# Attention decode on one Trainium2 core: keys loaded by pairs of units in 64 KB rows, at alternating offsets in one buffer

## The chip, the cores and the metric

The kernel runs on one core of one Trainium2 chip. The metric is the device time of one execution in microseconds; the kernel before takes 630.53 us (median of 3 runs, 630.49 to 630.74). A core has TensorE (PE; its weight loads are shown as PEld), VectorE (DVE), ScalarE (ACT), GpSimd (POOL) and SyncE (SP), and 16 DMA engines that move data between the chip's main memory (DRAM, HBM) and SBUF. TensorE writes into PSUM, from where VectorE and ScalarE read.

## The reference

One query for each of 32 heads attends over 65,536 keys; four query heads share one of 8 key/value heads. All tensors are bfloat16.

```python
B, Hq, Hkv, Sq, Sk, D = 1, 32, 8, 1, 65536, 128
...
def reference(q, k, v):
    B, Hq, Sq, D = q.shape
    Hkv = k.shape[1]
    rep = Hq // Hkv
    k = jnp.repeat(k, rep, axis=1)
    v = jnp.repeat(v, rep, axis=1)
    scale = D ** -0.5
    scores = jnp.einsum("bhqd,bhkd->bhqk", q, k) * scale
    p = _softmax(scores, axis=-1)
    return jnp.einsum("bhqk,bhkd->bhqd", p, v)
```

Keys and values are 134 MB each, and each is read once.

## The kernel before

A **unit** is a quarter of a head's keys: 128 x 128 = 16,384 keys, held as T = 128 tiles of 128 keys. There are NU = 32 units. A **round** handles two units, a (even) and b (odd), half a head; there are NR = 16 rounds, 0 to 15. In DRAM the 32,768 keys of a round are laid out so that each of the 128 partitions owns 256 consecutive keys, which are 64 KB in a row; unit a takes the first 32 KB of each partition's row and unit b the second.

**Loads (SP).** Keys go to two buffers of 128 tiles, `kbuf0` for a and `kbuf1` for b, by one DMA of 4 MB for each unit (128 rows of 32 KB; `load_k`, L406). Values of a whole round go to `vbuf` by one DMA of 8 MB (128 rows of 64 KB; `load_v`, L416). The order in SP's queue is: keys a, keys b, values, round after round. Before keys of a buffer are loaded again, SP waits for `kfree[b]`, which VectorE or ScalarE raises when it comes to the unit's last eviction (L204); before values it waits for `vfree`, raised when a round's values are summed (L298). The first unit's keys come in two halves, the values of round 14 and the keys of round 15 in halves, and the very last values in pieces (`V_PIECES`).

**Keys on TensorE.** For each group of TB = 8 tiles TensorE transposes the tiles into one of four PSUM buffers `trb` (`pe_transposes`, L117); the group is copied (evicted) to `ktb` in SBUF, three groups of four by VectorE and every fourth by ScalarE (`on_act`, L27; `evict`, L199); then 8 matmuls make its scores in `qkb` with the four queries as the moving operand (`pe_scores`, L128). Scores run LAG = 3 groups behind the transposes. A unit has G = 16 groups; TensorE waits for `krdy` ahead of a unit's first tile and for `khalf` at its middle.

**Softmax.** When a unit's scores are done (`qkd`), VectorE takes the maximum over its tiles (`scores_done`, L229), GpSimd reduces it over the partitions (L389), VectorE forms the running maximum (`maximum`, L239), and ScalarE makes four exponentials of 128 columns, one for each query head, with their sums, into `pts` (`exponentials`, L345). `exd` tells TensorE, and `sx` VectorE, that they are there. After a head's last unit VectorE first copies the next head's queries (`next_queries`).

**Values on TensorE.** For each unit 128 matmuls accumulate values times `pts` (`pe_values`, L158). TensorE's order in a round is: keys a, keys b, values a, values b (L190). VectorE rescales the accumulator `acc` by `alpha` and adds (L261 to L271), once for each unit. The round's order on VectorE is written out in `dve_round` (L273), on ScalarE in `act_round` (L358).

The last unit's values stand in `pe_last` (L165): they come in pieces; between them the sum over `lp` is taken, and then the last four rows are divided and stored.

Of the kernel before, what the change touches and what calls it, by code (L numbers as in the profile page):

```python
# [10 lines left out]
P = 128  # L11
T = 128
TB = 8
G = T // TB
# [4 lines left out]
HALF = T // 2  # L19
# [3 lines left out]

LOOP_SLOT = 176
# [18 lines left out]
def bass_standalone__gqa_softmax__decode_kernel(nc, q, k, v, out):  # L43
# [7 lines left out]

    NR, HALVES = NU // 2, HU // 2
    kf, vf, qf, of = k[0], v[0], q[0, :, 0, :], out[0, :, 0, :]
# [29 lines left out]
    rsum = sb("rsum", [P, R], DT.float32)  # L83
# [14 lines left out]
    fin = pvb[NU % 2]  # L98
# [18 lines left out]
    def pe_transposes(pe, b, j):  # L117
        kv = kbuf[b][:, :].rearrange("p (t d) -> p t d", d=D)
        for i in range(TB):
            t = j * TB + i  # L120
            if t == 0:
                take(pe, krdy[b], 16)
            if t == HALF:
                take(pe, khalf[b], 16)
            ins = pe.transpose(trb[j % NTB][:, i * P:(i + 1) * P], kv[:, t, :], ident[:, :])  # L125
        ins.then_inc(tra if on_act(j) else trd, 1)

    def pe_scores(pe, b, j):  # L128
        done, (k, last) = eva if on_act(j) else evd, turn(j)
        if j == 0:  # L130
            take(pe, qrdy)
        if last:
            take(pe, done, k)
        for i in range(TB):
            t, off = j * TB + i, (j % NKG * TB + i) * P
            ins = pe.matmul(qkb[b][:, t * R:(t + 1) * R], lhsT=ktb[:, off:off + P],  # L136
                            rhs=qcur[:, :], start=True, stop=True)
# [5 lines left out]
    def pe_keys(pe, b):  # L143
        pend = []
        for j in range(G):
            pe_transposes(pe, b, j)
            pend.append(j)
            if len(pend) > LAG:
                pe_scores(pe, b, pend.pop(0))
        while pend:  # L150
            pe_scores(pe, b, pend.pop(0))

    def value(pe, b, t, first, last):
        vv = vbuf[:, :].rearrange("p (t d) -> p t d", d=D)
        return pe.matmul(pvb[b][:, 0:R], lhsT=vv[:, b * T + t, :], rhs=pts[b][:, t * R:(t + 1) * R],  # L155
                         start=t == first, stop=t == last)

    def pe_values(pe, b):  # L158
        take(pe, vrdy[b], 16)
        take(pe, exd)  # L160
        for t in range(T):
            ins = value(pe, b, t, 0, T - 1)
        ins.then_inc(pvd, 1)

    def pe_last(pe):  # L165
        b = (NU - 1) % 2
        starts = [sum(V_PIECES[:i]) for i in range(len(V_PIECES))]
        pe.wait_ge(t_o, H - 1)
        pe.transpose(qkb[0][0:HR - R, 0:P], oT[:, R:HR], identf[:, :]).then_inc(s_o, 1)
        take(pe, exd)  # L170
        for t in range(T):
# [4 lines left out]
            ins = value(pe, b, t, 0, T - 1)  # L176
# [5 lines left out]
        ins.then_inc(s_fin, 1)  # L182

    def tensor_engine(pe):
# [14 lines left out]
    def evict(e, n, j):  # L199
        dst = ktb[:, j % NKG * TB * P:(j % NKG + 1) * TB * P]  # L200
        k, last = turn(j)
        if last:
            take(e, tra if on_act(j) else trd, k)
        if j == G - 1:  # L204
            e.sem_inc(kfree[n % 2], 1)
# [4 lines left out]
        if not last:  # L210
            ins.wait_op(tra if on_act(j) else trd, k, "sem-ge")
# [10 lines left out]
    PART = [[j for j in range(a, b) if not on_act(j)] for a, b in ((0, 4), (4, 12), (12, G))]  # L222

    def evictions(e, n, parts):
        for part in parts:
            for j in part:
                evict(e, n, j)

    def scores_done(e, u):  # L229
# [4 lines left out]
        else:  # L234
# [15 lines left out]
    def add_sums(e, u):  # L250

        take(e, sx)
        if u % HU == 0:
            own(e, e.tensor_copy(lp[:, :], rsum[:, :]), xd)
# [10 lines left out]
    def add_values(e, u):  # L265
        take(e, pvd)
        pv = pvb[u % 2][:, 0:R]
        if u % HU == 0:
            own(e, e.tensor_copy(acc, pv), xd)  # L269
        else:  # L270
            own(e, e.tensor_tensor(acc, acc, pv, ALU.add), xd)  # L271
# [24 lines left out]
    def values_done(e, u):  # L296
        add_values(e, u)
        e.sem_inc(vfree, 1)  # L298
# [23 lines left out]
    def vector_engine(e):  # L322
# [7 lines left out]
        with e.Fori(0, H) as h:  # L330
            for i in range(HALVES):
                dve_round(e, i, h)
        e.sem_inc(t_lp, 1)
        e.wait_ge(s_o, 1)
# [3 lines left out]
        ins = e.tensor_tensor(acc, acc, pvb[(NU - 1) % 2][:, 0:R], ALU.add)  # L338
# [6 lines left out]
    def exponentials(e, u):  # L345

        take(e, ng)
        e.activation(alpha[u % 2][:, :], dm[:, :], AF.Exp, scale=scale)  # L348
        sv = qkb[u % 2][:, :].rearrange("p (t g) -> p g t", g=R)
        pv = pts[u % 2][:, :].rearrange("p (t g) -> p g t", g=R)  # L350
        for g in range(R):
            ins = e.activation(pv[:, g, :], sv[:, g, :], AF.Exp, bias=negm[:, g:g + 1],  # L352
                               scale=scale, accum_out=rsum[:, g:g + 1])
# [4 lines left out]
    def act_round(e):  # L358
        for j in (3, 7, 11, 15):
            evict(e, 0, j)  # L360
        evict(e, 1, 3)
        exponentials(e, 0)
        for j in (7, 11, 15):
            evict(e, 1, j)
        exponentials(e, 1)

    def scalar_engine(e):
# [3 lines left out]
        with e.Fori(0, NR):  # L371
            act_round(e)
# [24 lines left out]
    def sync_engine(e):  # L397
        kp, vp, w = pairs(kf), pairs(vf), T * D

        def pieces(buf, s, sizes, sems):  # L400
            a = 0
            for n, sm in zip(sizes, sems):
                e.dma_start(buf[:, a * D:(a + n) * D], s[:, a * D:(a + n) * D]).then_inc(sm, 16)  # L403
                a += n

        def load_k(i, b, halves, first=False):  # L406
            if not first:
                take(e, kfree[b])
            s = kp[i][:, b * w:(b + 1) * w]
            if halves:  # L410
                pieces(kbuf[b], s, (HALF, T - HALF), (krdy[b], khalf[b]))
            else:
                e.dma_start(kbuf[b][:, :], s).then_inc(krdy[b], 16)
                e.sem_inc(khalf[b], 16)

        def load_v(i):  # L416
            e.dma_start(vbuf[:, :], vp[i]).then_inc(vrdy[0], 16)
            e.sem_inc(vrdy[1], 16)

        load_k(0, 0, True, first=True)  # L420
        load_k(0, 1, False, first=True)
        load_v(0)
        with e.Fori(1, NR - 2) as i:
# [55 lines left out]
```

## Time and profile before

| | |
|---|---|
| median of 3 runs | 630.53 us |
| the profiled execution | 630.56 us, its span (first to last instruction) 628.5 us |
| data read | 268.44 MB, 427 GB/s over the span |
| TensorE busy (matmul / weight load) | 78% / 77% of the span |
| VectorE, ScalarE, GpSimd busy | 50%, 30%, 3% |
| mean granted TensorE clock | 0.79 |

The head of the profile gives each engine's share of the span. Views by time list instructions merged: start in us from the span's start, duration in us, engine, source line, operation, output and input, count, and in square brackets the idle time of the engine ahead of it with what ended it. Views by group have total busy time and the mean of one in ns. The view of DMA issues has, for the issues of a stretch, size and median time from issue to landing. Windows give, for a stretch of time, the busy time of PE, PEld, DVE, ACT and POOL, the granted clock, the busy share of the DMA engines and GB/s. PEq, DVEq and so on are an engine's sequencer; L40 is the helper that waits for a semaphore.

### The profile page before, as it was taken

The numbers are of one execution on the slowest core, as the hardware profiler recorded it, in microseconds if no ns is written. First come the engines' busy times: TensorE is split into PE (matmuls) and PEld (weight loads), VectorE is DVE, ScalarE is ACT, GpSimd is POOL, SyncE is SP. The second block draws the span as 40 slices with busy tenths as digits, with TensorE's granted clock in tenths as the row PEclk, the third lists the DMA queues.
The fourth block names the chain that finished last, engine by engine and source line by source line (L and its number), as shares of the span: only waits on it lengthen the run. The fifth ranks groups of instructions, "written<-read, shape, count | busy, mean of one in ns | idle before, by whom it ended". The sixth has DMA issues, their size and how long they took to land. (4 is left out here: it accounts for less than half of the span.)

```text
span 628.5 us, 27046 instructions
## 1 busy us (share of the span) xinstructions
PE 489.2 (78%) x12293; PEld 482.3 (77%) x12293; DVE 312.5 (50%) x693; ACT 186.6 (30%) x418; POOL 16.4 (3%) x50
## 2 busy tenths in 40 slices
PE   4868859788696877967779686895868949689897
PEld 4758859687696877967679686895868949689896
DVE  4534726447273462725627256371563716537373
ACT  2321413314142141422414224041241413414141
POOL 0000000000000000000000000000000000000000
PEclk9776958769597695967959689696886969869596
DMA  8999999999999999999999999999999999999996
GB/s 369 439 426 446 434 415 453 415 453 430 419 448 419 448 419 434 453 413 455 407 432 438 425 438 430 430 455 409 455 413 438 442 415 448 417 434 432 423 444 283
DMA packets 8458, 268.58 MB, mean 427 GB/s; under 512 B 1026, under 2 KB 1282, under 8 KB 1538
## 3 DMA queue, kind: packets, MB, share of 16 engines
q1 hardware_dynamic: 8360, 268.44, 99.2%
q8 instruction: 7, 0.11, 0.1%
q10 hardware_dynamic: 90, 0.02, 0.0%
q14 instruction: 1, 0.01, 0.0%
HBM read 268.44 MB, written 0.01 MB: 427 GB/s over the span
## 5 line engine op out<-in xcount | busy, mean ns | idle before, releaser
L125 PE MATMUL trb<-ident,kbuf 128*128 128x128 bf16 x4096 | 328.3, 233 | 42.7 <-PEq L40 42.7
L209 DVE COPY ktb<-trb 128x1024 bf16<-128x1024 bf16 x384 | 254.2, 689 | 100.8 <-PE trb L125 97.5
L125 PEld LDWEIGHTS trb<-ident,kbuf 128*128 128x128 bf16 x4096 | 262.8, 105 | 43.7 <-issue 43.7
L207 ACT ACTIVATE ktb<-trb 128x1024 bf16<-128x1024 bf16 x128 | 131.1, 1024 | 379.1 <-PE trb L125 320.0
L136 PE MATMUL qkb<-qcur,ktb 128*128 128x4 bf16 x4096 | 170.9, 165 | 21.9 <-PEq L40 21.9
L136 PEld LDWEIGHTS qkb<-qcur,ktb 128*128 128x128 bf16 x4096 | 153.3, 97 | 26.0 <-issue 23.9
L155 PE MATMUL pvb<-pts,vbuf 128*128 128x4 bf16 x4096 | 112.3, 166 | 68.7 <-PEq L40 57.9
L155 PEld LDWEIGHTS pvb<-pts,vbuf 128*128 128x128 bf16 x4096 | 111.1, 104 | 70.1 <-issue 68.5
L352 ACT ACTIVATE pts<-qkb,negm 128x128 bf16<-128x128 f32 x128 | 50.5, 540 | 0.0
L236 DVE TENSOR_REDUCE cmax<-qkb 128x4 f32<-128x512 f32 x32 | 22.1, 692 | 43.2 <-DVEq L40 42.0
L271 DVE TENSOR_TENSOR acc<-acc,pvb 128x4 f32<-128x4 f32 x23 | 3.6, 158 | 62.8 <-DVEq L40 62.8
L352 ACT ACTIVATION_READ_ACCUMULATOR pts<-qkb,negm 128x1 f32 x128 | 34.6, 270 | 0.0
L389 POOL PARTITION_ALL_REDUCE cmaxa<-cmax x32 | 11.9, 372 | 576.3 <-POOLq L40 576.3
L348 ACT ACTIVATE alpha<-dm 128x4 f32<-128x4 f32 x32 | 6.6, 205 | 54.2 <-ACTq L40 53.4
L256 DVE TENSOR_TENSOR lp<-lp,alpha 128x4 f32<-128x4 f32 x24 | 3.8, 160 | 34.2 <-DVEq L40 34.2
L269 DVE COPY acc<-pvb 128x4 f32<-128x4 f32 x8 | 1.3, 162 | 25.5 <-DVEq L40 25.5
L246 DVE TENSOR_TENSOR m<-m,cmaxa 128x4 f32<-128x4 f32 x24 | 3.8, 159 | 11.5 <-DVEq L40 11.5
L218 DVE COPY qcur<-qT 128x4 bf16<-128x4 bf16 x9 | 1.5, 169 | 13.4 <-DVEq L40 13.3
L263 DVE TENSOR_TENSOR acc<-acc,alpha 128x4 f32<-128x4 f32 x24 | 3.9, 163 | 4.3 <-DVEq L40 1.9
L247 DVE TENSOR_TENSOR dm<-m 128x4 f32<-128x4 f32 x24 | 3.9, 162 | 3.5
L257 DVE TENSOR_TENSOR lp<-lp,rsum 128x4 f32<-128x4 f32 x24 | 3.9, 162 | 3.5
L391 POOL PARTITION_ALL_REDUCE la<-lp x8 | 3.4, 431 | 29.3 <-POOLq L40 29.3
(42 smaller groups left out, 23.7 us busy)
## 6 DMA issues: line engine op xcount, KB each, us to landing
kbuf<-in_k_dram SPq DMA_DIRECT2D x29, 4096.0 KB, 26.0
kbuf<-in_k_dram SPq DMA_DIRECT2D x6, 2048.0 KB, 21.1
vbuf<-in_v_dram SPq DMA_DIRECT2D x3, 4096.0 KB, 24.9
vbuf<-in_v_dram SPq DMA_DIRECT2D x1, 2048.0 KB, 29.4
vbuf<-in_v_dram SPq DMA_DIRECT2D x1, 1024.0 KB, 31.4
vbuf<-in_v_dram SPq DMA_DIRECT2D x1, 512.0 KB, 32.2
vbuf<-in_v_dram SPq DMA_DIRECT2D x1, 320.0 KB, 32.5
vbuf<-in_v_dram SPq DMA_DIRECT2D x14, 30.9
```

The costliest lines, as they stand in the source:

```text
L125: ins = pe.transpose(trb[j % NTB][:, i * P:(i + 1) * P], kv[:, t, :], ident[:, :])
L136: ins = pe.matmul(qkb[b][:, t * R:(t + 1) * R], lhsT=ktb[:, off:off + P], rhs=qcur[:, :], start=True, stop=True)
L155: return pe.matmul(pvb[b][:, 0:R], lhsT=vv[:, b * T + t, :], rhs=pts[b][:, t * R:(t + 1) * R], start=t == first, stop=t == last)
L207: ins = e.activation(dst, trb[j % NTB][:, :], AF.Copy).then_inc(eva, 1)
L209: ins = e.tensor_copy(dst, trb[j % NTB][:, :]).then_inc(evd, 1)
L236: e.tensor_reduce(cmax[:, :], qkb[u % 2][:, :].rearrange("p (t g) -> p g t", g=R), AX.X, ALU.max).then_inc(cm, 1)
L247: e.tensor_tensor(dm[:, :], mo[:, :], mn[:, :], ALU.subtract)
L257: own(e, e.tensor_tensor(lp[:, :], lp[:, :], rsum[:, :], ALU.add), xd)
L263: own(e, e.tensor_tensor(acc, acc, alpha[u % 2][:, :], ALU.mult), xd)
L348: e.activation(alpha[u % 2][:, :], dm[:, :], AF.Exp, scale=scale)
L352: ins = e.activation(pv[:, g, :], sv[:, g, :], AF.Exp, bias=negm[:, g:g + 1], scale=scale, accum_out=rsum[:, g:g + 1])
L389: e.partition_all_reduce(cmaxa[:, :], cmax[:, :], P, bass.bass_isa.ReduceOp.max).then_inc(cma, 1)
```

## The change

Keys of a round are loaded by one DMA of 8 MB with rows of 64 KB, as values were already, in rounds 1 to 13. The two key buffers become one `kbuf` of 320 tiles (T = 128, C = 64: 2T + C). Even rounds lie at tiles 64 to 319, odd rounds at 0 to 255. The 192 tiles 64 to 255 are common to both offsets. They are worked on first (GC = 24 groups); the other 64 tiles, at the end of an even round's stretch or at the beginning of an odd one's, come last, in 8 groups, by one of two branches on the round's parity. When the last common group is transposed, `kfree` lets SP load the next round's keys over them, at the other offset.

So that an odd round works on the common tiles first, its tiles are taken in a rotated order: `row_tile` gives the place in the row of the x-th tile, (x + 64) mod 256. Unit a of an odd round is places 64 to 191, unit b is places 192 to 255 and then 0 to 63, whose exponentials are made in two parts of 64 columns with sums of their own. `pts` is one buffer in the order of the row; values are accumulated by quarters q of 64 tiles into four column groups of `pvb[0]`, in the order 1, 0, 2, 3, where quarter 1 waits for the exponentials of a and quarter 0 for those of b. VectorE adds four quarters, with the rescale for b between them, and then raises `vfree`.

The groups of a round are counted through, G = 32. TensorE transposes groups 0 to 23 with scores three groups behind, finishes those scores, then transposes groups 24 to 31 (each from 28 on waits until the `trb` buffer is evicted) and then makes their scores. VectorE's maximum of unit a follows its evictions of groups 24 to 26, ScalarE's exponentials of a its eviction of group 27, ahead of group 31.

Round 0's keys come in parts of 64, 64 and 128 tiles, round 14's in two of 128, round 15's in four of 64; the values of round 14 come in halves and the last ones in a half and the same pieces as before. `pe_last` has the values of both units of round 15. The place of TensorE's loop in its code (`LOOP_SLOT`) changes from 176 to 80.

Bodies that are replaced stand in the listing of the kernel above.

```diff
+C = 64
...
-G = T // TB
+G = 2 * T // TB
+GA = T // TB
+GC = 3 * C // TB
...
-HALF = T // 2
...
-LOOP_SLOT = 176
+LOOP_SLOT = 80
...
+    def row_tile(odd, x):
+        return (x + C) % (2 * T) if odd else x
...
-    kbuf = [sb(f"kbuf{i}", [P, T * D], DT.bfloat16) for i in range(2)]
+    kbuf = sb("kbuf", [P, (2 * T + C) * D], DT.bfloat16)
...
-    pts = [sb(f"pts{i}", [P, T * R], DT.bfloat16) for i in range(2)]
+    pts = sb("pts", [P, 2 * T * R], DT.bfloat16)
...
-    rsum = sb("rsum", [P, R], DT.float32)
+    rsum = [sb(f"rsum{i}", [P, R], DT.float32) for i in range(3)]
...
-    krdy = [sem(f"krdy{i}") for i in range(2)]
-    khalf = [sem(f"khalf{i}") for i in range(2)]
...
+    krdy = [sem(f"krdy{i}") for i in range(2 * T // C)]
...
-    kfree = [sem(f"kfree{i}") for i in range(2)]
-    vfree = sem("vfree")
+    kfree, vfree = sem("kfree"), sem("vfree")
...
-    def pe_transposes(pe, b, j):
-        kv = kbuf[b][:, :].rearrange("p (t d) -> p t d", d=D)
+    def pe_transposes(pe, j, first):
+        if j * TB % C == 0:
+            take(pe, krdy[j * TB // C], 16)
...
+            t = first + i
+            ins = pe.transpose(trb[j % NTB][:, i * P:(i + 1) * P], kbuf[:, t * D:(t + 1) * D],
+                               ident[:, :])
+            if i == 0 and j >= GC + NTB:
+                ins.wait_op(eva if on_act(j - NTB) else evd, turn(j - NTB)[0], "sem-ge")
...
-    def pe_scores(pe, b, j):
+    def pe_scores(pe, j):
...
-            t, off = j * TB + i, (j % NKG * TB + i) * P
-            ins = pe.matmul(qkb[b][:, t * R:(t + 1) * R], lhsT=ktb[:, off:off + P],
+            t, off = (j * TB + i) % T, (j % NKG * TB + i) * P
+            ins = pe.matmul(qkb[j // GA][:, t * R:(t + 1) * R], lhsT=ktb[:, off:off + P],
...
-        if j == G - 1:
+        if j % GA == GA - 1:
...
+    def pe_keys(pe, i):
+        for j in range(GC + LAG):
+            if j < GC:
+                pe_transposes(pe, j, C + j * TB)
+            if j >= LAG:
+                pe_scores(pe, j - LAG)
+        with pe.If(i % 2 < 1):
+            for j in range(GC, G):
+                pe_transposes(pe, j, C + j * TB)
+        with pe.If(i % 2 > 0):
+            for j in range(GC, G):
+                pe_transposes(pe, j, j * TB - 3 * C)
+        for j in range(GC, G):
+            pe_scores(pe, j)
+    def value(pe, out, r, first, last):
+        return pe.matmul(out, lhsT=vbuf[:, r * D:(r + 1) * D], rhs=pts[:, r * R:(r + 1) * R],
+                         start=first, stop=last)
+    def pe_values(pe):
+        for q in (1, 0, 2, 3):
+            if q in (1, 2):
+                take(pe, vrdy[q - 1], 16)
+            if q in (1, 0):
+                take(pe, exd)
+            for r in range(q * C, (q + 1) * C):
+                ins = value(pe, pvb[0][:, q * R:(q + 1) * R], r, r % C == 0, r % C == C - 1)
+        ins.then_inc(pvd, 1)
+    def pe_last(pe):
+        starts = [sum(V_PIECES[:i]) for i in range(len(V_PIECES))]
...
+        pe.wait_ge(vrdy[0], 16)
+        for x in range(T):
+            ins = value(pe, pvb[0][:, 0:R], row_tile(True, x), x == 0, x == T - 1)
+        ins.then_inc(pvd, 1)
...
-            ins = value(pe, b, t, 0, T - 1)
+            ins = value(pe, pvb[1][:, 0:R], last_tile(t), t == 0, t == T - 1)
...
+    def last_tile(t):
+        return t if t < C else 2 * T - 2 * C + t
     def tensor_engine(pe):
...
-            pe_keys(pe, 0)
-            pe_keys(pe, 1)
-            pe_values(pe, 0)
+            pe_keys(pe, i)
...
-                pe_values(pe, 1)
+                pe_values(pe)
...
-    def evict(e, n, j):
+    def evict(e, j):
...
-        k, last = turn(j)
+        (k, last), done = turn(j), tra if on_act(j) else trd
...
-            take(e, tra if on_act(j) else trd, k)
-        if j == G - 1:
-            e.sem_inc(kfree[n % 2], 1)
+            take(e, done, k)
+        if j == GC - 1:
+            e.wait_ge(done, k)
+            e.sem_inc(kfree, 1)
...
-        if not last:
-            ins.wait_op(tra if on_act(j) else trd, k, "sem-ge")
+        if not last and j != GC - 1:
+            ins.wait_op(done, k, "sem-ge")
     def own(e, ins, s):
...
-    PART = [[j for j in range(a, b) if not on_act(j)] for a, b in ((0, 4), (4, 12), (12, G))]
...
+    def evictions(e, a, b):
+        for j in range(a, b):
+            if not on_act(j):
+                evict(e, j)
     def scores_done(e, u):
...
-        else:
+        elif u % 2:
...
-            own(e, e.tensor_tensor(lp[:, :], lp[:, :], rsum[:, :], ALU.add), xd)
+            for sums in ((rsum[0],), (rsum[1],), (rsum[0],), (rsum[1], rsum[2]))[u % HU]:
+                own(e, e.tensor_tensor(lp[:, :], lp[:, :], sums[:, :], ALU.add), xd)
...
+    def add(e, pv):
+        own(e, e.tensor_tensor(acc, acc, pv, ALU.add), xd)
+    def add_values(e, i):
+        rescale(e, 2 * i)
...
+        for n, x in enumerate(range(0, 2 * T, C)):
+            q = row_tile(i % 2, x) // C
+            pv = pvb[0][:, q * R:(q + 1) * R]
+            if x == T:
+                rescale(e, 2 * i + 1)
+            if i == 0 and n == 0:
+                own(e, e.tensor_copy(acc, pv), xd)
+            else:
+                add(e, pv)
+        e.sem_inc(vfree, 1)
     def dve_round(e, i, h):
...
-        evictions(e, a, PART)
+        evictions(e, 0, GC)
...
-        evictions(e, b, PART[:1])
+        evictions(e, GC, GC + NTB)
...
-        evictions(e, b, PART[1:2])
+        evictions(e, GC + NTB, G)
+        scores_done(e, b)
...
-        evictions(e, b, PART[2:])
-        scores_done(e, b)
...
-        rescale(e, a)
-        add_values(e, a)
-        rescale(e, b)
...
-            values_done(e, b)
+            add_values(e, i)
...
-                values_done(e, b)
+                add_values(e, i)
...
     def next_output(e):
...
+        rescale(e, NU - 2)
+        take(e, pvd)
+        add(e, pvb[0][:, 0:R])
...
+        rescale(e, NU - 1)
...
     def exponentials(e, u):
...
+        pv = pts[:, :].rearrange("p (t g) -> p g t", g=R)
+        odd, x = u // 2, u % 2 * T
+        if row_tile(odd, x + T - 1) == row_tile(odd, x) + T - 1:
+            parts = ((0, T, rsum[u % 2]),)
+        else:
+            parts = ((0, C, rsum[1]), (C, T, rsum[2]))
+        for a, b, sums in parts:
+            r = row_tile(odd, x + a)
+            for g in range(R):
+                ins = e.activation(pv[:, g, r:r + b - a], sv[:, g, a:b], AF.Exp,
+                                   bias=negm[:, g:g + 1], scale=scale, accum_out=sums[:, g:g + 1])
...
+    def act_round(e, i):
+        for j in range(GC + NTB):
+            if on_act(j):
+                evict(e, j)
+        exponentials(e, 2 * i)
+        for j in range(GC + NTB, G):
+            if on_act(j):
+                evict(e, j)
+        exponentials(e, 2 * i + 1)
     def scalar_engine(e):
...
-        with e.Fori(0, NR):
-            act_round(e)
+        with e.Fori(0, H):
+            for i in range(HALVES):
+                act_round(e, i)
...
     def sync_engine(e):
...
+        kp, vp = pairs(kf), pairs(vf)
+        def cols(a, b):
+            return slice(a * D, b * D)
+        def load_k(i, odd, parts=((0, 2 * T),)):
+            for a, b in parts:
+                r = row_tile(odd, a) if b - a < 2 * T else 0
+                n, f = b - a, r if odd else C + r
+                e.dma_start(kbuf[:, cols(f, f + n)], kp[i][:, cols(r, r + n)]).then_inc(krdy[a // C], 16)
+                for x in range(a + C, b, C):
+                    e.sem_inc(krdy[x // C], 16)
+        def load_v(i, ready, a, b):
+            e.dma_start(vbuf[:, cols(a, b)], vp[i][:, cols(a, b)]).then_inc(ready, 16)
+        def load_both(i, odd):
+            take(e, kfree)
+            load_k(i, odd)
+            take(e, vfree)
+            load_v(i, vrdy[0], 0, 2 * T)
...
+        load_k(0, 0, ((0, C), (C, 2 * C), (2 * C, 4 * C)))
+        load_v(0, vrdy[0], 0, 2 * T)
+        e.sem_inc(vrdy[1], 16)
+        load_both(1, 1)
+        with e.Fori(1, H - 1) as h:
+            load_both(2 * h, 0)
+            load_both(2 * h + 1, 1)
...
-        load_k(i, 0, False)
-        load_k(i, 1, False)
+        take(e, kfree)
+        load_k(i, 0, ((0, T), (T, 2 * T)))
...
+            load_v(i, vrdy[b], b * T, (b + 1) * T)
...
-        load_k(i, 0, True)
-        load_k(i, 1, True)
+        take(e, kfree)
+        load_k(i, 1, [(a, a + C) for a in range(0, 2 * T, C)])
...
+        load_v(i, vrdy[0], C, C + T)
+        t = 0
+        for n, sm in zip(V_PIECES, vpiece):
+            load_v(i, sm, last_tile(t), last_tile(t) + n)
+            t += n
```

More of the change, by code (lines that the diff above doesn't have):

```diff
@@ L139, in pe_scores @@
                 ins.wait_op(done, k, "sem-ge")
-        if j == G - 1:
+        if j % GA == GA - 1:
             ins.then_inc(qkd, 1)
[L143 to L161, printed above, removed]
-            ins = value(pe, b, t, 0, T - 1)
+    def pe_keys(pe, i):
[23 more added lines that the diff above has]
+                ins = value(pe, pvb[0][:, q * R:(q + 1) * R], r, r % C == 0, r % C == C - 1)
         ins.then_inc(pvd, 1)
     def pe_last(pe):
-        b = (NU - 1) % 2
         starts = [sum(V_PIECES[:i]) for i in range(len(V_PIECES))]
+        take(pe, exd)
         pe.wait_ge(t_o, H - 1)
         pe.transpose(qkb[0][0:HR - R, 0:P], oT[:, R:HR], identf[:, :]).then_inc(s_o, 1)
+        pe.wait_ge(vrdy[0], 16)
+        for x in range(T):
+            ins = value(pe, pvb[0][:, 0:R], row_tile(True, x), x == 0, x == T - 1)
+        ins.then_inc(pvd, 1)
         take(pe, exd)
@@ L397, in sync_engine @@
     def sync_engine(e):
[L398 to L414, printed above, removed]
@@ L416, in load_v @@
-        def load_v(i):
-            e.dma_start(vbuf[:, :], vp[i]).then_inc(vrdy[0], 16)
-            e.sem_inc(vrdy[1], 16)
[L420 to L423, printed above, removed]
-            load_k(i, 0, False)
-            load_k(i, 1, False)
-            take(e, vfree)
-            load_v(i)
+        kp, vp = pairs(kf), pairs(vf)
[8 more added lines that the diff above has]
+                    e.sem_inc(krdy[x // C], 16)
```

43 lines of the change are left out of this document (3 added, 40 removed).

## The prediction

> **What bounds the kernel now.** I read the page's head and its table of DMA queues first, then the chain that ended last, then one round (two units) in order of time, and at the end the last 110 us.
>
> ```profile
> span 628.5 us, 27046 instructions
> ...
> q1 hardware_dynamic: 8360, 268.44, 99.2%
> ...
> DMA vbuf<-in_v_dram 5%; SPq L403 0%; PE pvb L155 0%; PE pvb L180 0%; DVE olast L341 0%; SPq L438 0%; DVE acc L338 0%
> ```
>
> The SP queue's transfers fill 16 DMA engines for 99.2% of the span: the stream of keys and values is the bound, and all else hides behind it as long as each load is issued before the load ahead of it has ended. The rows of one round (round 4, with the end of round 3 ahead of it) show how much room there is:
>
> ```profile
> 155.43 0.34 PE L136 MATMUL qkb<-qcur,ktb 128*128 128x4 bf16 x8 [0.68 <-PEq L40]
> ...
> 160.13 0.28 ACT L352 ACTIVATION_READ_ACCUMULATOR pts<-qkb,negm 128x1 f32 x1
> ...
> 169.63 3.57 PE L125 MATMUL trb<-ident,kbuf 128*128 128x128 bf16 x32 [2.58 <-PEq L40]
> ...
> 173.24 0.61 PE L125 MATMUL trb<-ident,kbuf 128*128 128x128 bf16 x8
> ...
> 178.42 0.61 PE L125 MATMUL trb<-ident,kbuf 128*128 128x128 bf16 x8
> ...
> 181.16 1.02 ACT L207 ACTIVATE ktb<-trb 128x1024 bf16<-128x1024 bf16 x1 [1.72 <-ACTq L40]
> 181.32 0.33 SPq L413 DMA_DIRECT2D kbuf<-in_k_dram  x1
> 182.33 0.34 PE L136 MATMUL qkb<-qcur,ktb 128*128 128x4 bf16 x8 [0.69 <-PEq L40]
> ...
> 182.53 1.95 PE L125 MATMUL trb<-ident,kbuf 128*128 128x128 bf16 x32
> ...
> 192.59 0.33 SPq L413 DMA_DIRECT2D kbuf<-in_k_dram  x1
> 193.60 0.34 PE L136 MATMUL qkb<-qcur,ktb 128*128 128x4 bf16 x8 [0.69 <-PEq L40]
> ...
> 195.59 0.16 DVE L246 TENSOR_TENSOR m<-m,cmaxa 128x4 f32<-128x4 f32 x1 [0.72 <-DVEq L40]
> ...
> 196.37 0.53 ACT L352 ACTIVATE pts<-qkb,negm 128x128 bf16<-128x128 f32 x1
> ...
> 197.67 0.28 ACT L352 ACTIVATION_READ_ACCUMULATOR pts<-qkb,negm 128x1 f32 x1
> ...
> 198.85 6.97 PE L155 MATMUL pvb<-pts,vbuf 128*128 128x4 bf16 x256 [4.92 <-PEq L40]
> 202.56 0.16 DVE L269 COPY acc<-pvb 128x4 f32<-128x4 f32 x1 [3.81 <-DVEq L40]
> 202.87 0.16 DVE L263 TENSOR_TENSOR acc<-acc,alpha 128x4 f32<-128x4 f32 x1
> 205.97 0.16 DVE L271 TENSOR_TENSOR acc<-acc,pvb 128x4 f32<-128x4 f32 x1 [2.94 <-DVEq L40]
> 206.42 0.33 SPq L417 DMA_DIRECT2D vbuf<-in_v_dram  x1
> 208.41 3.57 PE L125 MATMUL trb<-ident,kbuf 128*128 128x128 bf16 x32 [2.59 <-PEq L40]
> ...
> 220.94 0.33 SPq L413 DMA_DIRECT2D kbuf<-in_k_dram  x1
> ```
>
> A round takes 208.41 − 169.63 = 38.8 us. From issue to landing, the three loads issued at 181.32, 192.59 and 206.42 took
>
> ```profile
> kbuf<-in_k_dram SPq DMA_DIRECT2D x1, 4096.0 KB, 27.0
> ...
> kbuf<-in_k_dram SPq DMA_DIRECT2D x1, 4096.0 KB, 25.4
> ...
> vbuf<-in_v_dram SPq DMA_DIRECT2D x1, 30.9
> ```
>
> so they landed at 208.3, 218.0 and 237.3. TensorE begins a round's keys 0.1 us after the first half has landed (208.41) and the second half comes 9.7 us later. Each load is issued some 11 us or more ahead of its turn (30.9 − 19.3 = 11.6 for values). That is the room which the change spends.
>
> **The change part by part.** *Rows of 64 KB.* 4 MB of keys in 32 KB rows take 9.7 us (218.0 − 208.3), 8 MB of values in 64 KB rows 19.3 (237.3 − 218.0). Twice 9.7 against 19.3 is at most 0.1 us a round, and 13 of the 16 rounds (1 to 13) change their rows: a gain of 0 to 1.3 us, taken as 1.0. On such merging the Trainium skill, DMA: Bandwidth & Descriptors, "Anatomy of one DMA", counts about 2.0 us fixed for every DMA (its path is GpSimd's, this one is SP's), by which 13 loads fewer would save an estimated 26 us. The trace does not agree for queued loads: they land at the pace of their bytes.
>
> *Keys start only when the whole pair has landed.* In rounds 1 to 13 one load of 8 MB signals the first key semaphore (SP sets the other three at once), so TensorE starts 9.7 us later against the stream. In the middle of the run that costs nothing by itself; it is late next at two places: the following loads, and the end.
>
> *The new round, from S, TensorE's first transpose.* Sixteen groups up to the issue that kfree allows take 181.32 − 169.63 = 11.7 or 220.94 − 208.41 = 12.5 us (TensorE's clock is low at first for a varying time); I take 12.1. Eight more groups at (178.42 − 173.24)/8 = 0.65 make 5.2: kfree after group 23 lets the next keys be issued at S+17.3. The flush of three score groups puts the next transpose 182.53 − 181.32 = 1.2 later, S+18.5. The two new branches are not in the trace; the loop's own way back is at most the 0.66 us in
>
> ```profile
> 53.19 1.12 PE L125 MATMUL trb<-ident,kbuf 128*128 128x128 bf16 x9 [0.66 <-PEq L40]
> ```
>
> so 0 to 0.66, taken as 0.3: S+18.8. Now eight groups are transposed ahead of their scores. VectorE needs about 2.7 us for three of their evictions (0.65 until the first can start, three of 0.69), and only then computes the maximum of unit a; maximum to last exponential is 195.59 to 197.95, 2.4 us; ScalarE evicts the last group only after those exponentials, hand-over 0.2; from that eviction to the last score is 181.16 to 182.67, 1.5. So 6.8, and the scores end at S+25.6 (before, 193.94 − 169.63 = 24.3 in a round with a short warm-up).
>
> Then unit b's exponentials: 193.94 to 197.95 = 4.0 us in an even round, 155.77 to 160.41 = 4.65 in an odd one (new queries are copied first). In odd rounds b is split in two: eight activations of 64 columns for four of 128 (1.58 us, 196.37 to 197.95). Half the width each costs between 0 (half the time) and 1.6 more (the same time); 0.95, since 1,024 columns take only 1.02 in L207, so 64 columns save under 0.07 each. The hand-over to TensorE is 0.26 (621.07 to 621.33, below). Only quarter 1 of the values can run earlier, for quarter 0 waits for both units: 192 matmuls remain at 6.97/256 us, 5.2. From TensorE's end to the issue of V is 206.42 − 205.82 = 0.6 with one addition; there are four operations more (three adds, one rescale) at 202.87 − 202.56 = 0.31: 1.85. V is issued at S+36.95 in even and S+38.5 in odd rounds; SP waits at vfree with nothing else queued that could fill the stream.
>
> *What a late issue costs.* No load of before was late but the first:
>
> ```profile
> 0.73 0.91 SPq L403 DMA_DIRECT2D kbuf<-in_k_dram  x2
> ...
> 0.73:1.83 1.10, 0.00 (x0) 0.00 (x0) 0.58 (x7) 0.65 (x1) 0.82 (x6) 1.00 0.01 2
> 1.83:2.75 0.92, 0.00 (x0) 0.00 (x0) 0.61 (x4) 0.84 (x2) 0.00 (x0) 1.00 1.04 292
> ...
> kbuf<-in_k_dram SPq DMA_DIRECT2D x1, 2048.0 KB, 7.4
> ```
>
> Nothing moves (DMA share 0.01) for 1.1 us after the issue, and 2 MB land after 7.4 us where their bytes at half of 9.7 need 4.9: a start into an empty queue costs 1.1 to 2.5, and I take the middle, 1.8. The stream needs V when the next keys have landed, S+38.7, less the 0.1 saved: S+38.6. Even rounds: 36.95 + 1.8 − 38.6 = 0.15 late. Odd rounds: 38.5 + 1.8 − 38.6 = 1.7 late. Of the value loads that delay round 13's keys, six follow odd and five follow even rounds: 6 × 1.7 + 5 × 0.15 = 11 us (6 at 1.1, 18 to 19 at 2.5). The keys' issue, 17.3 + 1.8 = 19.1, just meets the end of the values at S+19.2: 0, and at 2.5 it would be 0.6 late only where the values were not late themselves.
>
> *The end.* The page's chain ends in the last values' transfer. Before, TensorE began round 13 on half its keys:
>
> ```profile
> 518.62 1.65 PE L125 MATMUL trb<-ident,kbuf 128*128 128x128 bf16 x14 [2.60 <-PEq L40]
> ...
> 616.39 3.53 PE L155 MATMUL pvb<-pts,vbuf 128*128 128x4 bf16 x128
> ...
> 620.79 0.28 ACT L352 ACTIVATION_READ_ACCUMULATOR pts<-qkb,negm 128x1 f32 x1
> ...
> 621.33 1.85 PE L155 MATMUL pvb<-pts,vbuf 128*128 128x4 bf16 x64 [1.11 <-PEq L40]
> ...
> 623.57 0.19 PE L174 MATMUL pvb<-ones,lp 128*4 128x1 f32 x2 [0.39 <-DVEq L333]
> ...
> 623.69 2.26 PE L155 MATMUL pvb<-pts,vbuf 128*128 128x4 bf16 x64
> ```
>
> Now it begins at 518.62 + 9.7 = 528.3, and from there TensorE's own chain is the longer one: round 13 scores to 553.9, b's exponentials (4.65 + 0.95 + 0.26 = 5.85) to 559.8, values to 565.0; way back 0.3; round 14 590.9, 595.2, 600.4; round 15 from 600.7, 626.3, 632.1. The split loads of rounds 14 and 15 no longer help, since TensorE is still busy when they land. Then 128 values: the sum over lp came 623.57 − 621.07 = 2.5 after the exponentials and gets one more addition, 2.8; with the second 64 values (1.75) TensorE ends at 636.5, and 628.5 − 625.95 = 2.6 follow: 639.1 for 628.5, so 10.6 us. The last scores ended 10 us earlier before (616.43), and less than 1 us of that was slack.
>
> Sum against the profiled execution's 630.56 us (median of the runs 630.53, the same): 630.56 − 1.0 + 11 + 10.6 = 651.2, so **651 us**.
>
> **The rivals.** *Only the end is paid:* V comes in time in every round, if the split costs nothing and a queued start is cheap. For it: even rounds nearly manage. Time 630.56 − 1.0 + 10.6 = 640. *Both value loads late by a full cold start:* 2.5 for each, no gain from the split's shorter rows (1.6) and the branches at 0.66: odd 3.4, even 1.2, together 26, so 666. For it: the 7.4 us row; against: later loads find a queue that is just running out, not a cold one. *Faster:* the stream stays the bound to the end. It needs scores of the last round to end by some 617 us, as now, so TensorE would have to gain 9.6 us over three rounds; it has 2.6 us of idle ahead of each. If a shorter warm-up did that, 629.4; the only support is that such idle time exists. *A fixed price for each load that falls away:* at the 2.5 us of the first load, 13 fewer would save 32, 598; the landing times of queued loads speak against it. *The new branches fetch code:* the trace has one such hole in the first pass,
>
> ```profile
> PE pvb L155 <- issue: 1.8, 1, 1.8
> ```
>
> and two a round at 1.8 would be some 58 us on TensorE's chain, of which most shows: about 700. The Trainium skill, Runtime: NRT & Kernel Launch, "Instruction fetch mechanics", says a taken branch out of the fetched window stalls for a fetch; by that rule the loop's way back would show it too, and the trace, with its single hole, does not. *No change:* gain and cost cancel, 630.
>
> **How the numbers follow.** My forecast 0.63 (own range 646 to 660), end only 0.15, both late 0.10, code fetch 0.03, faster 0.05, fixed price 0.01, no change 0.03. A difference of 0.2% (1.3 us) is about what a measurement of this kernel can tell from no change. So slower 0.91, same 0.03, faster 0.06. The range takes in the end-only case and the upper bound of the start: 640 to 661.
>
> **What would show it.** SP's V issue 36 to 39 us after the first transpose of a round, later in odd rounds; rounds' starts alternately about 38.7 and 40.4 us apart; the DMA share under 99%, dropping in those places; 64 KB key loads at 19.3 us; the last scores near 636 us of the span (626 and the 10 of the stalls), with the chain of waits ending in scores, exponentials and values instead of a transfer. I am wrong if round starts stay 38.7 us apart (then 640), or if the final transfer still ends the chain (then 629).

## The result, and the profile after

The changed kernel takes 663.35 us (median of 6 runs, 661.58 to 666.43) against 630.53 for the kernel before: 1.0526 times the time, 95% interval 1.0496 to 1.0557. It is slower, as forecast, but by 32.8 us instead of the 20.5 forecast, and outside the predicted range. The profiled execution took 665.81 us.

The head of the changed kernel's page, its DMA queue, the chain that ended last and two groups of TensorE's:

```profile
span 663.9 us, 27035 instructions
...
q1 hardware_dynamic: 6488, 268.44, 95.6%
...
PE pvb L168 0%; PE pvb L201 0%; DVE olast L370 0%; PE pvb L195 0%; DVE acc L367 0%; DVEq L361 0%
...
L131 PE MATMUL trb<-ident,kbuf 128*128 128x128 bf16 x4096 | 318.7, 233 | 80.6 <-PEq L42 80.5
...
L168 PE MATMUL pvb<-pts,vbuf 128*128 128x4 bf16 x4096 | 113.3, 166 | 55.8 <-PEq L42 48.6
```

and the first of these groups before:

```profile
L125 PE MATMUL trb<-ident,kbuf 128*128 128x128 bf16 x4096 | 328.3, 233 | 42.7 <-PEq L40 42.7
```

A transpose takes 233 ns in both kernels, but TensorE's idle time ahead of the transposes grew from 42.7 to 80.6 us. The chain no longer has a transfer at its end. The queue is busy for 95.6% of a span that is 35.4 us longer. Its packets' time, as a mean over the 16 engines, is 0.956 × 663.9 = 634.7 us; before it was 0.992 × 628.5 = 623.5. So 11 us of the loss are not idle time: the same bytes took longer packets. The other 24 us are idle time of the DMA engines, 10 of them at the end, behind the last landing (at 650.7; before at 625.7).

Two stretches of the run, up to TensorE's first transpose on round 13's keys and from there (columns: busy time and instructions of PE, PEld, DVE, ACT, POOL, then the granted clock, the DMA share and GB/s), first after:

```profile
32.00:551.00 519.00, 376.22 (x9639) 370.62 (x9636) 241.51 (x555) 149.89 (x381) 12.27 (x32) 0.76 0.98 412
551.00:664.00 113.00, 94.70 (x2308) 92.86 (x2308) 59.47 (x136) 36.28 (x94) 3.10 (x8) 0.79 0.86 363
```

and before, where round 13's keys had wholly landed at 528.2:

```profile
32.00:528.00 496.00, 385.77 (x9799) 381.00 (x9797) 243.85 (x530) 145.83 (x327) 11.89 (x31) 0.78 1.00 432
528.00:628.50 100.50, 82.65 (x2121) 80.69 (x2118) 52.36 (x121) 31.69 (x76) 3.10 (x8) 0.79 0.95 407
```

So 23 us went in the rounds (519 for 496, with the same bytes: 412 × 519 is 432 × 496 within 0.3%) and 12.5 in the end. Two rounds in the middle, in order of time: first TensorE's transposes that open a round and SP's issues:

```profile
101.29 0.34 SPq L452 DMA_DIRECT2D vbuf<-in_v_dram  x1
...
103.22 3.57 PE L131 MATMUL trb<-ident,kbuf 128*128 128x128 bf16 x32 [3.76 <-PEq L42]
...
120.45 0.33 SPq L447 DMA_DIRECT2D kbuf<-in_k_dram  x1
...
127.81 0.34 PE L145 MATMUL qkb<-qcur,ktb 128*128 128x4 bf16 x8 [0.99 <-PEq L42]
...
139.53 0.33 SPq L452 DMA_DIRECT2D vbuf<-in_v_dram  x1
...
142.68 3.22 PE L131 MATMUL trb<-ident,kbuf 128*128 128x128 bf16 x32 [4.99 <-PEq L42]
...
159.14 0.33 SPq L447 DMA_DIRECT2D kbuf<-in_k_dram  x1
180.29 0.33 SPq L452 DMA_DIRECT2D vbuf<-in_v_dram  x1
...
183.90 1.33 PE L131 MATMUL trb<-ident,kbuf 128*128 128x128 bf16 x11 [5.44 <-PEq L42]
...
201.59 0.33 SPq L447 DMA_DIRECT2D kbuf<-in_k_dram  x1
```

then the time from issue to landing of the loads issued at 139.53, 159.14, 180.29 and 201.59:

```profile
vbuf<-in_v_dram SPq DMA_DIRECT2D x1, 22.4
...
kbuf<-in_k_dram SPq DMA_DIRECT2D x1, 24.6
...
vbuf<-in_v_dram SPq DMA_DIRECT2D x1, 24.1
...
kbuf<-in_k_dram SPq DMA_DIRECT2D x1, 22.1
```

By their last completion records they landed at 161.9, 183.8, 204.4 and 223.7, that is 21.9, 20.6 and 19.3 us after one another, where 19.35 would be the stream's pace. The values of 180.29 were issued 3.5 us ahead of the landing before them and still came 1.2 late; the keys of 159.14 were issued 2.8 ahead and came 2.5 late. That is what the forecast did not have. The landings of the keys of rounds 1 to 13, with which the rounds start, lie 39.5 to 42.2 us apart, 40.7 on average; the forecast had 38.7 and 40.4 in turn.

### The profile page after: what moved, and what is told of

It reads as the page before. It is cut to its first block, busy times and chain, and to the rows that moved or that the text cites. A ratio compares the mean times of both kernels' runs of the same rounds, so it can differ in the third digit from the quotient of the medians.

```text
span 663.9 us, 27035 instructions
## 1 busy us (share of the span) xinstructions
PE 490.0 (74%) x12293; PEld 482.3 (73%) x12293; DVE 316.6 (48%) x731; ACT 192.8 (29%) x482; POOL 16.4 (2%) x50
## 3 DMA queue, kind: packets, MB, share of 16 engines
q1 hardware_dynamic: 6488, 268.44, 95.6%
## 5 line engine op out<-in xcount | busy, mean ns | idle before, releaser
L131 PE MATMUL trb<-ident,kbuf 128*128 128x128 bf16 x4096 | 318.7, 233 | 80.6 <-PEq L42 80.5
L145 PE MATMUL qkb<-qcur,ktb 128*128 128x4 bf16 x4096 | 159.9, 165 | 29.6 <-PEq L42 15.9
L145 PEld LDWEIGHTS qkb<-qcur,ktb 128*128 128x128 bf16 x4096 | 144.9, 97 | 32.9 <-issue 18.4
L389 ACT ACTIVATE pts<-qkb,negm 128x128 bf16<-128x128 f32 (+1 forms) x160 | 57.7, 491 | 0.0
L389 ACT ACTIVATION_READ_ACCUMULATOR pts<-qkb,negm 128x1 f32 x160 | 40.3, 252 | 0.0
L258 DVE TENSOR_REDUCE cmax<-qkb 128x4 f32<-128x512 f32 x32 | 21.9, 686 | 19.3 <-DVEq L42 18.1
L289 DVE TENSOR_TENSOR acc<-acc,pvb 128x4 f32<-128x4 f32 x53 | 8.4, 158 | 35.4 <-DVEq L42 28.8
L242 DVE COPY qcur<-qT 128x4 bf16<-128x4 bf16 x9 | 1.5, 169 | 17.3 <-DVEq L42 17.2
L280 DVE TENSOR_TENSOR lp<-lp,rsum 128x4 f32<-128x4 f32 x32 | 5.4, 168 | 4.7
## 6 DMA issues: line engine op xcount, KB each, us to landing
vbuf<-in_v_dram SPq DMA_DIRECT2D x1, 2048.0 KB, 19.2
```

Of the source, the lines that this page charges most:

```text
L131: ins = pe.transpose(trb[j % NTB][:, i * P:(i + 1) * P], kbuf[:, t * D:(t + 1) * D], ident[:, :])
L145: ins = pe.matmul(qkb[j // GA][:, t * R:(t + 1) * R], lhsT=ktb[:, off:off + P], rhs=qcur[:, :], start=True, stop=True)
L258: e.tensor_reduce(cmax[:, :], qkb[u % 2][:, :].rearrange("p (t g) -> p g t", g=R), AX.X, ALU.max).then_inc(cm, 1)
L280: own(e, e.tensor_tensor(lp[:, :], lp[:, :], sums[:, :], ALU.add), xd)
L389: ins = e.activation(pv[:, g, r:r + b - a], sv[:, g, a:b], AF.Exp, bias=negm[:, g:g + 1], scale=scale, accum_out=sums[:, g:g + 1])
```

## The experiments

"Excess" below is the step from one 8 MB load's landing to the next, less 19.35. Each load has 16 completion records in the trace, one for each DMA engine; a landing is the last of them. "Ahead of the first engine" is the time from SP's issue to the first of the 16 completions of the load before.

**Keys in parts again, in the same buffer and order.** Each round's keys are loaded as 128, 64 and 64 tiles, with a semaphore for each part (the third quarter's by the round's parity).

```diff
+        PARTS = ((0, T), (T, T + C), (T + C, 2 * T))
...
-            load_k(i, odd)
+            load_k(i, odd, PARTS)
```

> The changed kernel with every round's keys loaded in three parts (128, 64 and 64 tiles, rows of 32 and 16 KB), so that TensorE may start a round when its first half has landed; buffer, offsets and order of work as changed. Theory A (the loss comes from TensorE starting 9.7 us later: late issues in the middle, a longer chain at the end): both go, 630 to 634 us, round starts 38.7 to 38.9 us apart. Rival B (transfers are slower for where they land, one shared buffer that TensorE reads at the same time): still above 645 us.

632.6 us, ratio 1.0034 (1.0022 to 1.0047). Nearly the whole loss is gone although the single buffer, the offsets, the new order, the split exponentials and the branches all stay. Its page shows the queue as busy as before:

```profile
span 630.2 us, 27083 instructions
...
q1 hardware_dynamic: 10520, 268.44, 99.2%
```

So none of these costs much: of the 1.5 us left in the profiled execution, 1.0 is in the rounds, at 38.86 us between landings for 38.78. What this run also takes back is the key load of 8 MB with rows of 64 KB; that such loads are not slow in themselves is shown by the kernel with less work, below. The two together leave the wait for the whole pair.

**The end alone.** Only the keys of rounds 13 and 14 come in these three parts.

```diff
-        with e.Fori(1, H - 1) as h:
+        with e.Fori(1, H - 2) as h:
             load_both(2 * h, 0)
             load_both(2 * h + 1, 1)
+        load_both(NR - 4, 0)
+        load_both(NR - 3, 1, PARTS)
```

> The changed kernel with the keys of round 13 alone (and of round 14, which came in halves already) in three parts. In the changed kernel's trace TensorE sits idle 6.7 us ahead of round 13. Theory A (the end is TensorE's own chain from round 13 on): those 6.7 us go, 655 to 658 us. Rival (the end hangs on the last transfers): no change, 662 to 664 us.

657.27 us (654.87 to 660.42), ratio 1.0437 (1.0407 to 1.0467): 6.1 us less than the change. In the change TensorE stood idle ahead of round 13 until all keys were there; here it goes straight on from its last values (the change first, then the experiment):

```profile
551.52 3.57 PE L131 MATMUL trb<-ident,kbuf 128*128 128x128 bf16 x32 [6.70 <-PEq L42]
```

```profile
539.85 1.07 PE L168 MATMUL pvb<-pts,vbuf 128*128 128x4 bf16 x35
540.88 3.43 PE L131 MATMUL trb<-ident,kbuf 128*128 128x128 bf16 x32
```

From that transpose to the end of the span it is 663.9 − 551.5 = 112.4 us in the one and 653.1 − 540.9 = 112.2 in the other: the end is TensorE's own chain from round 13 on, as long in the one as in the other although the loads land at different times.

**Values released earlier.** `vfree` is raised as soon as TensorE's values are done, ahead of VectorE's additions.

```diff
         take(e, pvd)
+        e.sem_inc(vfree, 1)
...
-        e.sem_inc(vfree, 1)
```

> The changed kernel with vfree raised when TensorE has finished the values, ahead of VectorE's additions: values are issued 1.5 us earlier in every round, some 36.8 us after a round's keys landed in odd rounds and 34.8 in even ones. Theory A as predicted (a load costs something only when it is issued less than 1.8 us ahead of the end of the load before it): the value loads' excess of 8.5 us goes and the keys cost no more than now, about 655 us. Rival C (a load has to be queued 3 us or more ahead, so the keys, issued 2.2 us ahead, pay too): what the values gain the keys lose, 660 to 668 us.

662.66 us (658.58 to 664.37), ratio 1.0491 (1.0449 to 1.0532): no gain that shows. The values were issued 4.6 us ahead of the last landing on average instead of 3.6, and their excess fell from 8.5 to 4.8 us in sum over 13 loads; the keys' rose from 15.7 to 17.2 over 12. A round whose values come earlier has its keys' issue fall closer to the end of them (2.5 us ahead instead of 3.0). Values issued 1 us earlier are not enough.

**Less work on TensorE.** Six of eight tiles of a group are transposed and evicted, and 16 of 64 values of a quarter are multiplied; all loads are as in the change.

```diff
-        for i in range(TB):
+        for i in range(TL):
             t = first + i
...
-            for r in range(q * C, (q + 1) * C):
+            for r in range(q * C, q * C + CL):
```

> The changed kernel with less work on TensorE: six of eight tiles of a group are transposed and evicted (the scores of the other two use tiles 0 and 1), and 16 of 64 values of a quarter are summed, except for the last round's values; all loads stay. Keys should be issued some 5 us ahead and values some 9. Theory A: no load is late, the end is the transfer again, and the wider rows show their own gain: 628.5 to 631 us, key loads landing 19.35 us apart from the values. Rival B (rows of 64 KB into the shared buffer are slower in themselves): above 640 us with key loads at 20 us or more.

630.33 us, ratio 0.9994 (0.9984 to 1.0003). The rounds are shorter, so every load is issued in time, and none has an excess. Its issues of one round, with the times to landing of the first two:

```profile
207.94 0.33 SPq L454 DMA_DIRECT2D vbuf<-in_v_dram  x1
232.08 0.33 SPq L449 DMA_DIRECT2D kbuf<-in_k_dram  x1
248.50 0.33 SPq L454 DMA_DIRECT2D vbuf<-in_v_dram  x1
```

```profile
vbuf<-in_v_dram SPq DMA_DIRECT2D x1, 29.3
...
kbuf<-in_k_dram SPq DMA_DIRECT2D x1, 24.5
```

The keys issued 237.2 − 232.1 = 5.2 us ahead landed 19.3 us after the values: no cost. A round takes 38.70 us between landings, for 38.78 before, so the longer rows gain 0.08 us a round, 1.0 in 13. That small gain does not show in the time: the last pieces of values took about 1 us longer here.

**The price of a late issue, in the kernel before.** Nothing is changed but one wait: SP holds each value load back until VectorE has come to group VJ of the next unit a. With VJ = 2, 6, 10 and 14 the margin shrinks step by step.

```diff
+        if n % 2 == 0 and j == VJ:
+            e.sem_inc(vgo, 1)
...
         def load_v(i):
+            take(e, vgo)
             e.dma_start(vbuf[:, :], vp[i]).then_inc(vrdy[0], 16)
```

> The kernel before, with one wait more: SP holds each load of values until VectorE has come to group 2 of unit a's keys, some 6 to 7 us ahead of the landing of unit b's keys (the load in front), instead of 11.6. Both theories: enough, 630 to 632 us. It is the zero of the scale.

> The same with group 6: values are issued some 3.4 us ahead of the landing of the keys in front, 1.4 us ahead of the first DMA engine's end (the 16 engines end 2 us apart). D1, the price as predicted (an issue costs only what it is less than 1.8 us ahead of the last landing): nothing, 630 to 632 us. D2 (it must lie about 2 us ahead of the first engine's end, and the last engine then pays as well, as the changed kernel's keys seem to): 1 to 2.5 us for each of 15 loads, 645 to 668 us.

> The same with group 10: issued some 0.8 us ahead of the last landing, 1.2 us after the first engine's end. D1: 1.0 us for each of 15 loads, about 645 us. D2: 2 to 3.5 us each, 660 to 683 us.

> The same with group 14: issued some 1.7 us after the last landing, so that all engines stand idle. D1: 1.7 + 1.8 = 3.5 us for each of 15 loads, about 683 us. D2 says the same here, or up to 1 us more for each, 683 to 698 us: with the queue empty both count a full start.

| VJ | issued ahead of last / first engine, us | excess of a load, us | time, us | ratio (95%) |
|---|---|---|---|---|
| 2 | 6.6 / 4.8 | 0.00 | 630.75 | 1.0004 (0.9995 to 1.0014) |
| 6 | 3.5 / 1.6 | 0.56 | 640.26 | 1.014 (1.011 to 1.017) |
| 10 | 0.8 / −0.15 | 1.95 | 659.67 | 1.045 (1.0428 to 1.0471) |
| 14 | −1.8 / −2.5 | 4.38 | 692.02 | 1.0968 (1.095 to 1.0987) |

With VJ = 6 the load is still issued 3.5 us before the load ahead of it has landed and costs 0.56 us each time; neither a price that begins only when the queue is empty nor a full start for every load fits. Two loads of this kernel, keys and then values (SP's issues, then the times to landing):

```profile
313.52 0.33 SPq L416 DMA_DIRECT2D kbuf<-in_k_dram  x1
335.10 0.33 SPq L421 DMA_DIRECT2D vbuf<-in_v_dram  x1
```

```profile
kbuf<-in_k_dram SPq DMA_DIRECT2D x1, 4096.0 KB, 25.6
...
vbuf<-in_v_dram SPq DMA_DIRECT2D x1, 23.8
```

The keys landed at 339.1, 4.0 us after the issue of the values, and the values at 358.9, 19.8 us later, not 19.35. With VJ = 14 the queue is empty for 1.8 us before the issue, and the excess beyond that is 4.38 − 1.82 = 2.56. Counted from the last landing, as the prediction counted it, that is the price of a start: about the 2.5 of the kernel's very first load, not the 1.8 that the prediction took. One such restart in that kernel, SP's issue and the stretches around it (columns as above):

```profile
236.89 0.33 SPq L421 DMA_DIRECT2D vbuf<-in_v_dram  x1
```

```profile
235.00:236.00 1.00, 1.00 (x31) 1.00 (x29) 0.72 (x2) 0.66 (x1) 0.00 (x0) 1.00 0.00 0
236.00:237.00 1.00, 1.00 (x27) 1.00 (x25) 0.93 (x2) 0.00 (x0) 0.00 (x0) 1.00 0.00 0
237.00:238.00 1.00, 0.86 (x28) 0.75 (x25) 0.38 (x1) 0.62 (x1) 0.00 (x0) 1.00 1.60 524
```

A packet counts where it starts. None starts until the stretch from 237: the trace's packets have the first at 237.85, 0.96 us after the issue, and fifteen of the sixteen engines' first 64 KB packets take 2.9 to 3.4 us where all later ones take 2.42. The load landed 22.0 us after its issue, at 258.9, and the load ahead of it at 234.6: of the 24.3 us between, 19.35 are the stream's pace and 2.3 the time until the issue, so this start cost 2.7. An engine waited 1.2 us on average for its first packet, which took 0.7 longer, and its last packet of the load before had ended on average 0.8 ahead of the last landing: with the 2.3 until the issue these are 5.0 us, which is 24.3 − 19.35 within 0.05. The start itself is 1.9 of them for each engine.

**Keys issued earlier as well.** On top of the earlier `vfree`, the first 128 tiles of the next keys are released at group 15 and the rest at group 23. TensorE still waits for the whole pair in rounds 1 to 13, so the end stays.

```diff
-        if j == GC - 1:
+        if j in (GA - 1, GC - 1):
             e.wait_ge(done, k)
-            e.sem_inc(kfree, 1)
+            e.sem_inc(kfree if j == GC - 1 else kfa, 1)
...
         def load_both(i, odd):
+            take(e, kfa)
+            part(i, odd, 0, T, krdy[1])
             take(e, kfree)
```

> The run with the early vfree, and in rounds 1 to 15 the keys are issued in two steps: the first 128 tiles of the next round when group 15 is transposed (5 us earlier, some 7 us ahead of the landing of the values in front), the rest when group 23 is. TensorE still starts rounds 1 to 13 only when all their keys have landed. Theory C (the keys of the changed kernel pay for being queued only 2 to 4 us ahead): the key loads' excess, 17 us in the run with the early vfree, goes; the values, some 1.7 us ahead in odd rounds and 3.4 in even ones, still pay 1.3 and 0.6 by the delayed-values runs (11 us), the end its 12, shorter rows up to 2: 653 to 657 us. Rival (the key loads are slower for another reason than their issue): 660 to 664 us.

649.58 us (647.83 to 653.76), ratio 1.0316 (1.0273 to 1.0359): 13 us less than with the earlier `vfree` alone, and 3 us below the range expected: the values, 2 us ahead in every second round, keep 5.4 us in sum, where 11 were expected. Keys are now issued 7 us or more ahead and have no excess at all. They also come in two or three loads here instead of one, but a load of 4 MB pays too when it is late: the first half of round 14's keys in the changed kernel, issued 2.5 us ahead, landed 11.35 us after the load before instead of 9.71. The queue's share rises:

```profile
span 647.6 us, 27102 instructions
...
q1 hardware_dynamic: 9368, 268.44, 96.9%
```

No version of the changed kernel with all of its work beat the kernel before; the nearest is the first one, with the keys in parts, at 632.6.

## Why the prediction was right and wrong

**Sign and places: right.** The stream is what waits, in the rounds and at the end, and TensorE's chain ends the run. The two new branches, a rival at 700 us, are not what costs: with them in place the version with keys in parts is 2 us from the kernel before. In the changed kernel TensorE has two holes in front of its value matmuls that end in no recorded wait, 2.1 and 3.8 us, both in the first round; the kernel before has one of 1.8.

**Rows of 64 KB, gain 1.0:** right in size (0.08 us a round, shown by the kernel with less work), though it was not seen in a time.

**The new round:** right. Keys' issue was forecast 17.3 us after a round's first transpose: 120.45 − 103.22 = 17.2. The end of the scores, forecast at 25.6, came at 128.15 − 103.22 = 24.9. The issue of V was forecast at 36.95 us in even rounds and 38.5 in odd ones: 139.53 − 103.22 = 36.3, and 101.29 in the round whose first transpose was at 62.93, 38.4 later. Eight half-width exponentials took 2.46 us (654.37 to 656.83) against 1.58 for four (130.59 to 132.17), 0.88 more for a forecast of 0.95 (the prediction's own working, 8 × 0.07 off 1.6, gives 1.04). By these times nothing should have been worse than forecast.

**What a late issue costs: this is the step that failed.** It took 1.8 us for a start, counted from the landing of the load ahead, and so no cost for any load issued 1.8 us or more before that. The runs with a held-back value load show otherwise: 0.56 us at 3.5 ahead, 1.95 at 0.8 ahead, 4.38 at 1.8 behind, and nothing only from about 5 us on. By the price of the prediction none of the 25 loads counted below, issued 1.8 to 4.7 us ahead, would have cost anything; they cost 24.2 us. Two things were missed. The sixteen engines don't end together: in the changed kernel the first is done 0.5 to 3.5 us before the last, and an engine that has run dry waits for itself (an estimate on this reading, in the last section, fits the traces). And an engine that finds its queue empty has a longer first packet besides, which is most of the 11 us of added packet time on the page: 391 of the changed kernel's 3,456 packets of 64 KB took over 2.5 us, 12.0 us too long in all as a mean over the engines, and 10.6 of these stand in packets that started within 4 us of SP's issue of a load. In the kernel before three packets of that size were so long.

**So the keys' term, forecast 0, was the large one.** "The keys' issue, 17.3 + 1.8 = 19.1, just meets the end of the values at S+19.2": in the run it was 3.0 us ahead of the last engine, 1.0 ahead of the first, and the twelve key loads lost 15.7 us. The value loads lost 8.5 where 11 were forecast. That this is near is luck: the late keys gave them time, so that they were issued 3.6 us ahead of the last landing on average and not 0.1 to 1.65, and at that margin the prediction counted nothing. By the mean of the engines' completions, which shares a straggler's delay more evenly, it is 13.0 for keys and 10.6 for values. That the two trade is what the earlier `vfree` showed: it took from the one and gave to the other. That the keys' issue carries a large part is shown by the last run, where earlier keys brought 13 us on top of the earlier `vfree`; earlier keys without the earlier `vfree` were not run.

**The end, 10.6:** right in mechanism, measured 12.2 (112.5 from the landing of round 13's keys to the end, 100.3 before). The sum had 25.6 us from a round's first transpose to its last score. Round 13 took 25.1, rounds 14 and 15 took 27.1 each (round 15's window):

```profile
624.20:651.30 27.10, 25.38 (x513) 25.09 (x512) 17.57 (x33) 9.78 (x17) 0.37 (x1) 0.83 0.94 398
```

That is 2.5 us too much over the three rounds; the rest of the chain, with the exponentials and the values, was 0.9 shorter than forecast, which leaves the missing 1.6.

**The sum.** 630.56 + 24.2 (15.7 + 8.5) − 1.0 + 12.2 = 666.0 for the profiled 665.81. The rival "both value loads late by a full cold start" named 666 too, but for another reason: it put all of it on values and nothing on keys, and its 26 us of values were 8.5.

**What stays open.** Why single engines straggle by up to 3.5 us after a late issue, and why the excess of single landings is spread so unevenly (0 to 2.5 us for loads issued 2.7 to 3 us ahead), is not settled. The trace shows packets and completions, not how an engine gets its next descriptors.

## What to carry to other kernels

A load that is to keep a stream full has to be issued well before the load ahead of it ends, because some DMA engines finish well before the last; here 5 us ahead of the last landing was free, and 3 was not. When a change merges loads or moves a release, list the margin of every load in the loop, and treat one that "just meets" as late at the full price. Before merging two loads, look for who starts on the first half: that overlap was worth some 30 us here, the longer rows 1.

## What was not expected of the hardware

The delay of an 8 MB load, as the mean over its 16 engines, follows its margin against the first engine's end nearly in one curve, through ten kernels (the one before, the changed one and all experiments but the first), with values and keys alike:

| issued ahead of the first engine's end, us | loads | mean delay, us |
|---|---|---|
| −3.3 to −3 | 3 | 4.9 |
| −3 to −2 | 8 | 4.4 |
| −2 to −1 | 6 | 3.4 |
| −1 to −0.3 | 3 | 2.2 |
| −0.3 to 0.3 | 24 | 1.8 |
| 0.3 to 0.8 | 11 | 1.4 |
| 0.8 to 1.3 | 17 | 1.0 |
| 1.3 to 2 | 13 | 0.6 |
| 2 to 3 | 27 | 0.14 |
| over 3 | 65 | 0.02 |

At a margin of 0 the price is 1.8 us, by chance the number that the prediction took, which counted from another point. The margin against the mean of the engines' ends gives as narrow a curve (a scatter of 0.2 us about it either way), so that the first engine is the better mark is not shown; against the last engine the scatter is 0.55. An estimate from these 177 loads: if each engine pays 2.3 us less its own lead, which is the time from SP's issue to the engine's completion record of the load before, and never less than 0, the mean delays come out with a scatter of 0.2 us. On a fixed cost of about 2 us the Trainium skill, DMA: Bandwidth & Descriptors, "Anatomy of one DMA", says that most of it is the wait for the written data's receipt at the end of a DMA (for GpSimd's path; this is SP's). The restart above shows a price at the front, 0.96 us from the issue to the first packet and, in fifteen of the sixteen first packets, 0.4 to 1.0 us more; from the end of an engine's last packet to its completion record it is 0.4 us on average there. A load issued early enough hides all of it (0.00 us with VJ = 2).
